# Where the convolution's matmul groups stand: gate chains, filter block 3 and block 2's inverse, and the order of the opening

## The chip, the cores and the metric

The kernel runs on one core of one Trainium2 chip. The metric is the device time of one execution in microseconds (us). Of the kernel before, three executions were timed, and one further execution was recorded by the hardware profiler. The engines are TensorE (PE in the profile, its weight loads PEld), VectorE (DVE), ScalarE (ACT), GpSimd (POOL) and SyncE (SP). Each runs its own instructions in program order and waits on semaphores for the others. POOL and SP also issue the DMAs.

## The reference

Two layers alternate, each a long convolution with a gate (A) and a GeGLU feed-forward (B), for 2048 tokens of width 576, hidden width 4608. Both layers use the same A_k, A_v and filters, so the convolution `y` is the same in both, and only its gate `q` differs. Abridged:

```python
def _A_ref(q, k, v, shift_k, ssm_k, ssm_D):
    k_shift = sum of k_pad[:, t:t+S, :] * shift_k[:, ks-1-t]        # ks = 4
    kv = k_shift * v
    y = irfft(rfft(pad(kv)) * rfft(pad(ssm_k)))[:S]                 # causal, length 2S
    return q * (y + kv * ssm_D)

def _B_ref(x, w_gate, w_up, w_down):
    return (gelu(x @ w_gate) * (x @ w_up)) @ w_down

x = A_q
for layer in range(2):
    x = x + _A_ref(layernorm(x), A_k, A_v, A_shift_k, A_ssm_k, A_ssm_D)
    x = x + _B_ref(layernorm(x), B_w_gate, B_w_up, B_w_down)
```

## The kernel before

**Units and visits.** Tokens are cut into four chunks c = 0 to 3 of 512. A unit is (layer, chunk), u0 = (0,0), u1 = (0,1), u2 = (1,0), u3 = (1,1), u4 = (0,2), u5 = (0,3), u6 = (1,2), u7 = (1,3). The feed-forward runs in five passes, [u0], [u1, u2], [u3, u4], [u5, u6], [u7], and each pass goes three times through a third of the hidden width. One third of one unit is called a visit here, numbered 0 to 23 in the order in which they run: u0 has visits 0 to 2; u1 and u2 alternate in 3 to 8, u3 and u4 in 9 to 14, u5 and u6 in 15 to 20; u7 has 21 to 23. A visit is first 216 matmuls for gate and up (`gu`, L1376, 12 tiles of 18), each tile followed by the gelu on ACT (L1380) and the product on DVE (L1381); then 96 matmuls down (`dn`, L1393), for each of the four token tiles j 24 of them, whose sum DVE adds to `x_c` (L1429, in a unit's last visit L1424 with a row sum, or L1415 into the output tile). PSUM has three buffers in pool `psp`, for `gu` and `dn`, and one in `cpsp`, for the convolution.

**The convolution** is a block transform of four blocks of 512 tokens, written as matmuls with twiddle tables `W` and `Wx`. Class `Conv` holds deques of its steps: `Pq` (matmul groups), `V` and `U` (DVE steps), `L` (loads and transposes). `filt(b)` transforms block b of the filter in eight small groups (`quarter`, L254: two matmuls into `cps`, then an ACT copy to an `eo` buffer, of which there are N_EO = 4); the DVE closures `both`, `even` and `odd` combine four `eo` buffers. `step(m)` does block m: the shift and product (`kv_ops`), its transform (again `quarter` for m > 1), the products with the filter blocks (`prod`, `add`), `cross` and `shift`, which writes `z` (L306), and the inverse, four groups of eight matmuls (`inverse`, L325) whose result ACT copies to `y` (L331). `self.neo` counts the `eo` buffers in use. In the program the order is filter 2, block 2, filter 3, block 3.

**The order around the feed-forward** is fixed when the program is built, by a planner with a clock for each engine (`Pace`: `t.pe`, `t.dve`, `t.act`, with costs such as `C_R4`). After each `gu` tile and each pair of `dn` matmuls it calls `fill(limit, tensor, conv_first)`, which issues loads, DVE steps, ACT steps (`aq`) and, where `tensor` is true, groups from `Pq` by `run_p`. `tensor` is true in the `dn` part, and in the `gu` part when `now()` says so.

**Gate chains.** When chunk c's `y` and `x` are there, the tasks of `prep` (deque `vq`) make the gate of the convolution layer and the next layer norm, for each of four tiles: `x_c` times gate (L1040, L1047 on DVE), mean (`nm`, L1004 on POOL), squares (`junk`, L1012 on ACT), `ve` and `rstd` (L1019, L1020 on POOL), the normed tile `xn` (L1073 on DVE), and two DMA transposes by SP into `xnT` (L1103), from which the unit's `gu` matmuls read. For a layer-1 unit the chain starts in the `dn` part of the layer-0 unit's last visit; for u4 and u5 it starts when block 2's or block 3's inverse is there.

**The opening** (`begin`, L674 to L884) is written out by hand: block 0 of filter and input, products `kacc(kt)` into `A[(part, kt)]`, sums and differences `pair0(kt, sg)` into `yb` (L799), four inverses `inv0(mt)` into PSUM tiles `Y[mt]`, then the gates of the first four tiles (`gate0`, L1236 and L1239), norms (L1189), PE transposes (`turn0`, L1205) and copies (`copy0`, L1212), up to the first `gu` matmul (L1308). `stats(j)` (L970 to L978) makes mean and variance of tiles 0 and 1 of `x_b`. SP issues the loads of the opening one after the other.

Of the kernel before, what the change touches and what calls it, by code (L numbers as in the profile page):

```python
# [17 lines left out]
F32 = mybir.dt.float32  # L18
# [4 lines left out]
P = 128  # L23
# [3 lines left out]
RT = BS // P  # L27
# [14 lines left out]
AHEAD = 3.0  # L42
# [41 lines left out]
class Conv:  # L84
# [9 lines left out]
    def __init__(self, tc, ctx, pace, A_k, A_v, A_shift_k, A_ssm_k, A_ssm_D, ident, psp, cpsp, ypool):  # L94
# [30 lines left out]
        self.h1_at = {2: 0.0}  # L125
        self.load_at, self.tight = -9.0, lambda: False
# [77 lines left out]
    def fwd_full(self, src, kt, s, dst, copy=None, ps=None):  # L204
# [6 lines left out]
        (copy or nc.scalar.copy)(out=self.halves(dst[:, s, :]), in_=ps[:, :, 0:HW])  # L211
# [13 lines left out]
    def quarter(self, src, out, h, ready, seen, done):  # L225
# [90 lines left out]
    def inverse(self, m, mt, terms, ps=None):  # L316
# [6 lines left out]
        for n, (lhs, z) in enumerate(terms):  # L323
            for h in range(2):
                nc.tensor.matmul(ps[:, h, 0:HW], lhsT=lhs, rhs=z[:, h * HW:(h + 1) * HW],  # L325
                                 start=(n == 0), stop=(n == len(terms) - 1))
# [41 lines left out]
    def filt(self, b):  # L368
# [23 lines left out]
        for h in range(2):  # L392
            self.Pq.extend(self.quarter(lambda: own["t"], out, h, lambda: own.get("at", NEVER), seen, done))

    def step(self, m, kv=None, loaded=False):
# [186 lines left out]
        for mt in range(RT):  # L582
            self.Pq.append((lambda: max(zs(), self.y_used.get(m - 2, NEVER) if m > 1 else 0.0), 0.98, inv(mt)))
# [34 lines left out]
    def run_p(self, other=False):  # L618
# [4 lines left out]
        ready, cost, run = self.Pq[0]  # L623
# [50 lines left out]
    def begin(self, head, tables):  # L674
# [4 lines left out]
        with ExitStack() as es:  # L679
# [88 lines left out]
            def h_part(b, kt, s, copy=None, ps=None):  # L768
# [7 lines left out]
                self.fwd_full(src, kt, s, t, copy, ps)  # L776
                if s == 1 and b == 0:
                    self.flush(0.0)
                    self.spill(self.Hd[b][kt], t)

# [26 lines left out]
            taps(DBS[0])  # L807
            turn_h(0, hT0, 0)
# [33 lines left out]
            head.stats(0)  # L842
# [3 lines left out]
            head.stats(1)  # L846
# [6 lines left out]
            h_part(1, 2, 0)  # L853
            self.flush(0.0)
# [629 lines left out]
```

## Time and profile before

| what | us |
|---|---|
| timed executions | 936.36, 938.77, 939.27 |
| median | 938.77 |
| profiled execution, its own time | 936.63 |
| its span | 934.9 |
| PE busy in it | 917.5 |
| DVE busy | 589.0 |
| ACT busy | 291.9 |
| POOL busy | 143.5 |

The span runs from the first to the last instruction; 1.7 us lie around it. In the profile's lines a matmul's duration is longer than the distance to the next one, since matmuls overlap; an idle time in square brackets is that of the engine just before the line's first instruction, with what ended it. Windows give the busy time of each engine in a stretch, and the clock that TensorE was granted as a share of full speed.

### The profile page before, as it was taken

Reading aid. Unit: us, or ns where it says so; the run is one execution under the profiler, and the core shown is the slowest. Engines: PE = TensorE matmul, PEld = TensorE weight load, DVE = VectorE, ACT = ScalarE, POOL = GpSimd, SP = SyncE. Lnnn points to the kernel's source line nnn. Section 1 sums busy time; section 2 is a strip of 40 time slices with the busy share of each in tenths; the row PEclk is TensorE's granted clock in tenths of the full one; section 3 lists DMA queues with packets and bytes.
Section 4 is the critical chain, followed back from the end, with each engine's and each line's share of the span. In section 5 each row is a group of like instructions: output and inputs, shape, how many; then the busy total and the mean of one; then the engine's idle time right before and its main releaser. Section 6 shows DMA issues by size and latency. Waiting matters only on the chain.

```text
span 934.9 us, 19345 instructions
## 1 busy us (share of the span) xinstructions
PE 917.5 (98%) x8248; PEld 536.7 (57%) x8249; DVE 589.0 (63%) x1051; ACT 291.9 (31%) x538; POOL 143.5 (15%) x305
## 2 busy tenths in 40 slices
PE   9899998999999999999999999899999999999998
PEld 6786555465565565664654655646556556556555
DVE  6888977677569888677698896653333335433332
ACT  6663224423224233332324122431221223311211
POOL 2433003201013131121014110320000002100000
PEclk9999999999999999999999999989999999999999
DMA  9978978909329717647725913650720730787720
GB/s 257 344 191 251 178 181 165 249 31 261 103 76 188 223 42 139 154 115 185 183 65 131 238 59 90 120 122 19 147 84 1 143 87 13 137 206 159 146 65 26
DMA packets 128490, 130.25 MB, mean 139 GB/s; under 512 B 43538, under 2 KB 120339, under 8 KB 128404
## 3 DMA queue, kind: packets, MB, share of 16 engines
q1 hardware_dynamic: 119232, 93.47, 46.6%
q0 software_dynamic: 9168, 35.54, 11.3%
q8 instruction: 64, 1.05, 0.5%
q14 instruction: 22, 0.18, 0.1%
q10 hardware_dynamic: 4, 0.01, 0.0%
HBM read 107.76 MB, written 11.80 MB: 128 GB/s over the span
## 4 chain that ended last, share of the span: by engine, by line
PE 93%; DVE 3%; POOL 2%; issue 1%; ACT 1%; DMA 0%; SPq 0%; DVEq 0%
PE gu L1376 58%; PE dn L1393 28%; PE gu L1308 3%; PE cps L325 1%; PE cps L254 1%; POOL rstd L1020 1%; PE cps L219 1%; DVE x_c L1424 0%; POOL ve L1019 0%; DVE yb L287 0%; ACT junk L1012 0%; POOL nm L1004 0%; DVE prod L286 0%; PE ps L209 0%; DVE yb L799 0%
## 5 line engine op out<-in xcount | busy, mean ns | idle before, releaser
L1376 PE MATMUL gu<-xnT,wgu 64*128 64x512 bf16 x4968 | 544.0, 377 | 5.9 <-DMA xnT<-xn 5.4
L1376 PEld LDWEIGHTS <-wgu 64*128 64x128 bf16 x4968 | 242.8, 94 | 300.3 <-issue 15.9
L1380 ACT ACTIVATE ga<-gu 128x512 f32<-128x512 f32 x276 | 164.8, 597 | 522.5 <-PE gu L1376 504.2
L1381 DVE TENSOR_TENSOR hT<-ga,gu 128x512 bf16<-128x512 f32 x276 | 189.2, 686 | 210.6 <-ACT ga L1380 209.4
L1393 PE MATMUL dn<-wd,hT 128*128 128x288 bf16 x2304 | 294.3, 286 | 0.5 <-DVE ob L1402 0.5
L1393 PEld LDWEIGHTS <-hT 128*128 128x128 bf16 x2304 | 223.5, 98 | 66.1 <-issue 10.5
L1429 DVE TENSOR_TENSOR x_c<-x_c,dn 128x576 f32<-128x576 f32 x64 | 48.1, 752 | 59.9 <-PE dn L1393 59.8
L1004 POOL TENSOR_SCALAR nm<-s 128x1 f32<-128x1 f32 x62 | 24.6, 397 | 299.3 <-DVE x_c L1424 170.2
L1012 ACT ACTIVATE junk<-x_c,nm 128x576 bf16<-128x576 f32 x48 | 37.0, 770 | 34.1 <-POOL nm L1004 34.0
L451 POOL DMA_DIRECT2D hr<-Hd x32 | 17.3, 542 | 149.9 <-DVE prod L286 149.9
L1020 POOL TENSOR_TENSOR rstd<-ve,neghalf_t 128x1 f32<-128x1 f32 x62 | 38.2, 617 | 5.2
L256 ACT COPY eo<-cps 128x576 f32<-128x576 f32 x32 | 20.4, 637 | 31.6 <-PE cps L254 31.6
L1415 DVE TENSOR_TENSOR ob<-x_c,dn 128x576 bf16<-128x576 f32 x15 | 11.3, 754 | 23.9 <-PE dn L1393 18.2
L1308 PE MATMUL gu<-xnT,wgu 64*128 64x256 bf16 x432 | 24.8, 269 | 0.5 <-DVE xnT L1212 0.5
L1308 PEld LDWEIGHTS <-wgu 64*128 64x128 bf16 x432 | 21.2, 94 | 3.5 <-issue 1.5
L287 DVE TENSOR_TENSOR prod<-prod 128x576 bf16<-128x576 bf16 x48 | 22.0, 458 | 1.7
L1019 POOL TENSOR_SCALAR ve<-ss 128x1 f32<-128x1 f32 x62 | 17.9, 289 | 30.8 <-ACT junk L1012 30.6
L1073 DVE TENSOR_SCALAR xn<-x_c,nm,rstd 128x576 bf16<-128x576 f32 x28 | 16.1, 576 | 4.5 <-POOL rstd L1020 4.4
L529 DVE TENSOR_TENSOR zs<-zs,prod 128x576 f32<-128x576 f32 x24 | 18.1, 754 | 0.3
L526 DVE TENSOR_TENSOR zs<-sum,prod 128x576 f32<-128x576 bf16 x24 | 18.1, 753 | 0.3
L184 DVE TENSOR_TENSOR kvt<-k,skc 128x1152 bf16<-128x1152 bf16 x24 | 17.7, 753 | 0.2
L340 POOL DMA_DIRECT2D out_dram<-ob x12 | 6.7, 556 | 72.8 <-DVE ob L1415 70.1
(138 smaller groups left out, 538.1 us busy)
## 6 DMA issues: line engine op xcount, KB each, us to landing
wgu<-in_B_w_gate_dram SPq DMA_DIRECT2D x45, 576.0 KB, 5.6
wd<-in_B_w_down_dram SPq DMA_DIRECT2D x30, 864.0 KB, 7.0
wgu<-in_B_w_up_dram SPq DMA_DIRECT2D x45, 512.0 KB, 7.9
hr<-Hd POOLq DMA_DIRECT2D x32, 288.0 KB, 5.5
kr<-Kd POOLq DMA_DIRECT2D x24, 288.0 KB, 6.0
Kd<-kc POOLq DMA_DIRECT2D x12, 288.0 KB, 4.5
k<-in_A_k_dram POOLq DMA_DIRECT2D x3, 1008.0 KB, 7.0
wgu<-in_B_w_up_dram SPq DMA_DIRECT2D x45, 64.0 KB, 7.3
```

The source lines that it names most:

```text
L256: nc.scalar.copy(out=A[i][:], in_=ps[:, :, 0:HW])
L287: nc.vector.tensor_tensor(out=dst, in0=pr[:, 0, :], in1=pr[:, 1, :], op=ALU.subtract if part == 0 else ALU.add)
L526: nc.vector.tensor_tensor(out=f[:], in0=self.halves(pr0[:]), in1=self.halves(pr[:]), op=ALU.add)
L1004: nc.gpsimd.tensor_scalar(out=v["nm"][:], in0=v["s"][:], scalar1=-1.0 / D, scalar2=None, op0=ALU.mult)
L1012: nc.scalar.activation(out=junk[:], in_=get_x(), func=ACT.Square, bias=v["nm"][:, 0:1], accum_out=v["ss"][:])
L1020: nc.gpsimd.tensor_tensor(out=v["rstd"][:], in0=ve[:], in1=neghalf_t[:, 0:1], op=ALU.pow)
L1308: nc.tensor.matmul(pair[:, s, e * 256:(e + 1) * 256], lhsT=w[r0:r0 + HK, k, gi * P:(gi + 1) * P], rhs=xnT[r0:r0 + HK, blk_of[k], tok], sta ...
L1376: nc.tensor.matmul(pair[:, s, :], lhsT=w[r0:r0 + HK, k, gi * P:(gi + 1) * P], rhs=xnT[r0:r0 + HK, b, :], start=(k == 0), stop=(k == NKC - 1))
L1380: nc.scalar.activation(out=ga[:], in_=pair[:, 0, :], func=ACT.Gelu_apprx_tanh)
L1381: nc.vector.tensor_tensor(out=hT[:, fi, :], in0=ga[:], in1=pair[:, 1, :], op=ALU.mult)
L1393: nc.tensor.matmul(acc[:, h, 0:HW], lhsT=hT[:, fi, at * P:(at + 1) * P], rhs=wd[2 * wb + fi // WT][:, fi % WT, h * HW:(h + 1) * HW], start ...
L1429: nc.vector.tensor_tensor(out=xh, in0=xh, in1=acc[:, :, 0:HW], op=ALU.add)
```

## The change

It has three parts.

1. **Groups and gate chains.** `fill` lets a group out of `Pq` only when the planner's clock is past `conv.ps_free`, and 2.5 us (`CHAINED`) past it while `chained()` holds, that is while ACT steps are queued or the head of `vq` is anything but a gate whose `y` is not there yet. The wait does not hold as long as block 1's inverse is not done. `conv.tight`, which spaces the loads, is the same test.
2. **Filter 3 ahead of block 2's inverse.** The four inverse groups of block 2 are kept in `self.then` and put into `Pq` behind filter 3's groups, which in turn wait until `z` of the block before is there (`z_at`). In `quarter` the groups come in the order 0, 1, 2, 3; the next four may start when two `eo` buffers are free again (`odd` and `even` give back two each, `odd` first), where before the first of them waited for all four. `wanted()` lets block 2's inverse out in the `gu` part too when the head of `vq` waits for it.
3. **Opening.** `x_b` is loaded ahead of `W` and `Wx` on SP's queue, and `stats(0)` and `stats(1)` come before the second shift product. `straight(mt)` forms inverses 0 and 2 from the products `A` themselves, six terms in place of four (12 matmuls in place of 8), and the first eight matmuls of inverse 0 come ahead of the filter's part `h_part(1, 2, 0)`. `pair0(1, 0)` is moved to the end of the opening. `Y[3]` goes to `psp` in place of `cpsp`, `h_part(1, 2, 0)` to `cpsp`, the DVE copy of `h_part(1, 2, 1)` is issued separately (`rest`), and the second transpose tile of `turn0` goes to `cpsp`.

```diff
-AHEAD = 3.0
+AHEAD, CHAINED = 3.0, 2.5
...
         def even():
...
+            self.neo -= 2
             done(0, h, t.on_dve(2 * C_R4) + LAG)
         def odd():
...
-            self.neo -= RT
+            self.neo -= 2
...
+                    self.U.append((when + LAG, 4 * C_BF, odd))
                     self.U.append((when + LAG, 2 * C_R4, even))
-                    self.U.append((when + LAG, 4 * C_BF, odd))
...
-        return [(lambda i=i: max(ready(), NEVER if self.neo >= (N_EO if i else 1) else 0.0), 0.25, one(i)) for i in (0, 2, 1, 3)]
+        return [(lambda: max(ready(), NEVER if self.neo >= N_EO else 0.0), 0.25, one(i)) for i in range(RT)]
...
-            self.Pq.extend(self.quarter(lambda: own["t"], out, h, lambda: own.get("at", NEVER), seen, done))
+            self.Pq.extend(self.quarter(lambda: own["t"], out, h, lambda: max(own.get("at", NEVER), self.z_at[b - 1]()), seen, done))
+        self.Pq.extend(self.then)
+        self.then = []
...
-        for mt in range(RT):
-            self.Pq.append((lambda: max(zs(), self.y_used.get(m - 2, NEVER) if m > 1 else 0.0), 0.98, inv(mt)))
+        self.z_at[m] = zs
+        out = [(lambda: max(zs(), self.y_used.get(m - 2, NEVER) if m > 1 else 0.0), 0.98, inv(mt), m) for mt in range(RT)]
+        if m == 2:
+            self.then = out
+        else:
+            self.Pq.extend(out)
...
             self.load_v(0, nc.sync)
+            head.more(0)
             nc.sync.dma_start(out=self.W[:, 0:12, :], in_=tables[:, 0:12, :])
             nc.sync.dma_start(out=self.Wx[:], in_=tables[:, 24:26, :])
-            head.more(0)
...
+            def straight(mt):
+                w, odd = self.inv_w, [(s, kt) for kt in (1, 3) for s in range(2)]
+                return [(w(mt, s), self.yb[(s, 0, 0)]) for s in range(2)] + [(w(mt, s, mt == 2), A[(s, kt)]) for s, kt in odd]
...
             taps(DBS[0])
+            head.stats(0)
+            head.stats(1)
             turn_h(0, hT0, 0)
...
             pair0(0, 0)
-            head.stats(0)
             tile(1)
             kacc(1)
             pair0(0, 1)
-            head.stats(1)
             tile(3)
...
             kacc(3)
-            h_part(1, 2, 0)
-            self.flush(0.0)
-            pair0(1, 0)
             Y = {mt: self.psp.tile([P, 2, 512], F32, tag="pr", name="ps") for mt in (2, 1, 0)}
             small = lambda: self.cpsp.tile([P, 2, 512], F32, tag="cps", name="cps")
-            inv0(0, Y[0])
-            inv0(2, Y[2])
+            near = {mt: straight(mt) for mt in (0, 2)}
+            self.inverse(0, 0, near[0][:4], Y[0], True, False)
+            h_part(1, 2, 0, None, small())
+            self.flush(0.0)
             pair0(1, 1)
+            self.inverse(0, 0, near[0][4:], Y[0], False, True)
+            self.inverse(0, 2, near[2], Y[2])
+            rest = h_part(1, 2, 1, nc.vector.tensor_copy, small(), True)
             inv0(1, Y[1])
             head.gate(0, Y[0])
             head.mean(0)
             self.keep_y(0, 2, Y[2])
-            self.keep_y(0, 1, Y[1])
+            Y[3] = inv0(3, self.psp.tile([P, 2, 512], F32, tag="pr", name="ps"))
...
             self.keep_y(0, 3, Y[3])
+            pair0(1, 0)
             self.startup = False
...
+    def chained():
+        need = vq[0][0] if vq else None
+        return bool(aq) or need is not None and not (need[0] == "y2" and need[1:3] not in conv.y_at)
...
-        if tensor:
+        if tensor and (hurry() or t.pe > conv.ps_free + (CHAINED if chained() else 0.0)):
             for _ in range(3):
                 if not conv.run_p():
                     break
...
-            pt.append(new() if two else pt[0])
+            pt.append(cpsp.tile([P, 2, 1024], BF16, tag="cps", name="xps") if two else pt[0])
...
-        now = lambda: hurry() and (t.pe > 60.0 or conv.fresh > 0)
-        conv.tight = lambda: bool(vq or aq)
+        def wanted():
+            need = vq[0][0] if vq else (None,)
+            return conv.Pq and len(conv.Pq[0]) > 3 and need[0] == "y2" and need[1:3] not in conv.y_at
+        now = lambda: wanted() or hurry() and (t.pe > 60.0 or conv.fresh > 0)
+        conv.tight = chained
```

In the built program the change moves matmuls as follows, against the order before. In visit 2's `dn` part one of three filter groups (L254) is left, after 74 of the 96 `dn` matmuls; the two others come in visit 3. Block 2's transform ends in visit 4 (before: visit 5). Filter 3's groups come in visits 7 and 8 (before: 8 and 9), block 2's inverse stays in visit 8, behind them. Block 3's transform comes in visits 8 and 9 (before: 10), and block 3's inverse in visit 13 (before: visit 14). On DVE block 3's last `z` stands ahead of nine of the twelve L1381 of visit 13. On SP's queue u5's eight transposes now come in visit 14, ahead of two sets of gate and up weights (L944 to L946) that stood before them. On POOL's queue the first six loads of block 3's products (`kr`, `hr`) stand ahead of and between the first steps (`nm`, `ve`, `rstd`) of u4's chain.

More of the change, by code (lines that the diff above doesn't have):

```diff
@@ L125, in __init__ @@
         self.h1_at = {2: 0.0}
+        self.z_at, self.then = {}, []
         self.load_at, self.tight = -9.0, lambda: False
@@ L202, in kv_ops, with fwd_full @@
         return ops
-    def fwd_full(self, src, kt, s, dst, copy=None, ps=None):
+    def fwd_full(self, src, kt, s, dst, copy=None, ps=None, later=False):
         nc = self.nc
@@ L210, in fwd_full @@
                                  start=(n == 0), stop=(n == RT - 1))
-        (copy or nc.scalar.copy)(out=self.halves(dst[:, s, :]), in_=ps[:, :, 0:HW])
+        run = lambda: (copy or nc.scalar.copy)(out=self.halves(dst[:, s, :]), in_=ps[:, :, 0:HW])
+        return run if later else run()
     def fwd_eo(self, src, kt, s, h, scale=1.0):
@@ L314, in terms, with inverse @@
         return out + [(w(mt, 0, mt == 1), z[(1, 1, sg)]), (w(mt, 1, mt == 3), z[(0, 1, sg)])]
-    def inverse(self, m, mt, terms, ps=None):
+    def inverse(self, m, mt, terms, ps=None, first=True, last=True):
         nc = self.nc
@@ L325, in inverse @@
                 nc.tensor.matmul(ps[:, h, 0:HW], lhsT=lhs, rhs=z[:, h * HW:(h + 1) * HW],
-                                 start=(n == 0), stop=(n == len(terms) - 1))
+                                 start=(first and n == 0), stop=(last and n == len(terms) - 1))
         if own:
@@ L622, in run_p @@
             return False
-        ready, cost, run = self.Pq[0]
+        ready, cost, run = self.Pq[0][:3]
         if max(ready(), 0.0 if other else self.ps_free) > t.pe:
@@ L766, in begin, with h_part @@
             h0, kc, A = {}, {}, {}
-            def h_part(b, kt, s, copy=None, ps=None):
+            def h_part(b, kt, s, copy=None, ps=None, later=False):
                 if b == 1:
@@ L775, in h_part @@
                     t, src = h0[kt], hT0
-                self.fwd_full(src, kt, s, t, copy, ps)
+                run = self.fwd_full(src, kt, s, t, copy, ps, later)
                 if s == 1 and b == 0:
```

7 lines of the change are left out of this document (4 added, 3 removed).

## The prediction, made before the changed kernel had run

> **What bounds the kernel now.** The page comes first: span, engines, clock.
>
> ```profile
> span 934.9 us, 19345 instructions
> PE 917.5 (98%) x8248; PEld 536.7 (57%) x8249; DVE 589.0 (63%) x1051; ACT 291.9 (31%) x538; POOL 143.5 (15%) x305
> ...
> PEclk9999999999999999999999999989999999999999
> ```
>
> TensorE is the bound almost everywhere; DVE has over a third of its time free. So the change can win only where PE stands idle or runs slowly, and it wins nothing by moving matmuls about. There are 17.4 us of idle PE in the span, and one slice whose clock is below 9. I then read PE's timeline around each idle time, and the chain of waits for the length of an undisturbed visit. The largest is at the start of visit 15, u5's first:
>
> ```profile
> 596.31 8.00 PE L1393 MATMUL dn<-wd,hT 128*128 128x288 bf16 x64
> 609.27 0.61 PE L1376 MATMUL gu<-xnT,wgu 64*128 64x512 bf16 x2 [4.95 <-DMA xnT<-xn]
> 610.34 4.02 PE L1376 MATMUL gu<-xnT,wgu 64*128 64x512 bf16 x18 [0.46 <-DMA xnT<-xn]
> ```
>
> ```profile
> 565.11 23.42 PE gu L1376 x216
> ...
> 636.25 11.87 PE dn L1393 x96
> ```
>
> The `dn` matmuls end at 596.31 + 8.00 = 604.31, and the next `dn` part begins at 636.25, so visit 15's 216 `gu` matmuls took 31.94 where 23.42 is usual: **8.52 us lost**. Only 5.41 of it is idle time. The rest is the clock:
>
> ```profile
> core 0: us, PE busy (x) PEld busy (x) DVE busy (x) ACT busy (x) POOL busy (x), PEclk, DMA share, GB/s
> 604.30:609.30 5.00, 0.05 (x3) 0.06 (x2) 2.90 (x7) 1.15 (x4) 2.85 (x7) 0.96 0.54 106
> 609.30:614.00 4.70, 4.24 (x20) 1.65 (x22) 0.00 (x0) 0.00 (x0) 0.00 (x0) 0.50 0.86 249
> 614.00:618.00 4.00, 4.00 (x32) 1.79 (x30) 2.75 (x5) 2.49 (x5) 0.89 (x3) 0.78 0.53 177
> 160.00:166.00 6.00, 3.07 (x26) 2.14 (x26) 4.07 (x9) 3.16 (x7) 3.85 (x9) 1.00 0.92 179
> ```
>
> After the idle time TensorE is granted half speed (0.50, then 0.78). Its cause is that block 3's inverse runs only in visit 14, the last before u5 starts, so u5's whole gate chain and eight transposes are squeezed into one `dn` part, beside u6's.
>
> The second idle time stands in visit 2:
>
> ```profile
> 159.53 1.14 PE L1393 MATMUL dn<-wd,hT 128*128 128x288 bf16 x8
> 163.61 0.40 PE L254 MATMUL cps<-hT,W 128*128 128x288 bf16 x2 [2.93 <-ACT eo L256]
> ```
>
> ```profile
> 162.17 0.78 ACT L1012 ACTIVATE junk<-x_c,nm 128x576 bf16<-128x576 f32 x1 [2.81 <-POOL nm L1004]
> ...
> 162.94 0.62 ACT L256 COPY eo<-cps 128x576 f32<-128x576 f32 x1
> ```
>
> A filter group waits for the one `cps` buffer. Its copy stands on ACT behind a `junk` that waits 2.81 us for u2's gate chain. The clock stayed at 1.00 (last row of the windows), so this one costs its 2.93 and no more.
>
> [...]
>
> **Term 1: block 3's inverse a visit earlier.** In the built order it stands in visit 13, 35.3 us (23.42 + 11.87) earlier, and DVE's last `z` nine tiles of visit 13, some 17 us, ahead of it. u5's gates then stand in the `gu` part of visit 14, as u4's do in visit 9 (386 to 422) now, where PE is busy throughout:
>
> ```profile
> 386.00:422.00 36.00, 36.00 (x322) 20.38 (x320) 27.07 (x51) 12.73 (x24) 9.82 (x22) 1.00 0.52 136
> ```
>
> The eight transposes end over 10 us before visit 15. So the 8.52 go. What is late next is u6's chain, alone now, in visit 14's `dn` part. Its DVE order is the one that u7's chain has now in visit 19, so I take that row's price, **+0.49**:
>
> ```profile
> 793.73 6.63 PE L1376 MATMUL gu<-xnT,wgu 64*128 64x512 bf16 x59 [0.49 <-DVE x_c L1424]
> ```
>
> Bounds: 0 and 2.93, the other chain's wait. No matmul is added in the visits. By counting each visit's DVE instructions at their durations, the fullest visit has about 30 us of DVE work after the change and 29 before, of 35.3. That cover holds both the earlier products and the hT products on which PE waits.
>
> **Term 2: fewer groups in visit 2's `dn` part.** One of three is left, and its buffer was freed long before. PE then reaches visit 3 2.93 earlier, near 163.0. What could be late there is u1's `xnT`, or the tile buffer that the last L1424 frees:
>
> ```profile
> 155.50 3.89 SPq L1103 DMA_TRANSPOSE xnT<-xn  x3
> ...
> DMA to landing us min/median/max: 2.5/3.5/6.0
> ```
>
> ```profile
> 162.18 0.75 DVE L1424 SCALAR_TENSOR_TENSOR x_c<-dn,x_c 128x576 f32<-128x576 f32 x1
> ...
> 163.27 0.82 DVE L1040 SCALAR_TENSOR_TENSOR g_t<-x_c,nm,y 128x576 f32<-128x576 f32 x1 [0.33 <-POOL nm L1004]
> ```
>
> The third transpose is issued near 158.1 and lands at 161.6 by the median, 164.1 by the worst. The fourth tile's L1424 follows the L1040 at 163.27 and ends near 164.8; the third `gu` tile needs that buffer at 163.0 + 2 × 1.95 = 166.9. So **-2.93**, at worst -1.8. The two groups moved to visit 3 cost PE the same there as here.
>
> **Term 3: the opening.** DVE sets the pace from 18 us to the first gates.
>
> ```profile
> 28.41 0.81 DVE L970 BATCH_NORM_STATS2 stats<-x_b 128x6 f32<-128x288 bf16 x2
> ...
> 29.62 0.75 DVE L283 TENSOR_TENSOR prod<-kc,h 128x1152 bf16<-128x1152 bf16 x1
> ...
> 32.01 1.56 DVE L799 TENSOR_TENSOR yb<-yb 128x576 bf16<-128x576 bf16 x4
> 33.49 0.81 DVE L1236 SCALAR_TENSOR_TENSOR x_c<-x_b,mv,ps 128x576 f32<-128x576 bf16 x1
> ...
> 39.39 0.57 DVE L1189 TENSOR_SCALAR xn<-x_c,nm,rstd 128x576 bf16<-128x576 f32 x1
> ```
>
> ```profile
> 27.65 0.64 ACT L211 CAST kc<-ps 128x576 bf16<-128x576 f32 x1 [0.34 <-PE ps L209]
> 28.52 2.14 ACT L764 COPY hT<-hps 128x1152 bf16<-128x1152 bf16 x2 [0.24 <-PE hps L763]
> 34.31 0.65 ACT L331 ACTIVATE y<-ps 128x576 bf16<-128x576 f32 x1 [2.03 <-PE ps L325]
> ```
>
> ```profile
> 27.45 2.03 PE L763 MATMUL hps<-ident,hn 128*128 128x128 bf16 x20
> ...
> 41.14 1.08 PE L1308 MATMUL gu<-xnT,wgu 64*128 64x256 bf16 x14 [0.45 <-DVE xnT L1212]
> ```
>
> Two statistics of 1.21 us each (28.41 to 29.62) leave this stretch. The last products (29.62) cannot follow by 2.42, since their input is copied at 27.65 + 0.64 = 28.29; they start at 28.33 and end at 30.80 (2.47 later, as 29.62 to 32.09 now). PE: transposes end at 29.48; eight matmuls of inverse 0 at 0.122 each (from the 64 of the same shape in 8.00, whose last ends 0.29 after its start) end at 30.46; the filter part's eight wait for the second `hT` copy (30.66) and end at 31.45; the four last of inverse 0 end near 32.1. So the first L1236 starts at 32.15 in place of 33.49. Inverse 2's twelve end near 33.6, its `y` copy at 34.3 in place of 34.96, and the second gate starts 0.8 earlier. From there nm, squares and `rstd` follow as now; the second L1189 waits for its `rstd` near 38.45 in place of 39.39, and transposes, copies and the first L1308 follow 0.94 earlier: **-0.94**. The eight matmuls added lie in idle PE time ahead of that gate. Without that cover they cost 0.98. `Y[3]` in `psp` holds the third `gu` tile alone, whose buffer is copied out by then. Bounds: +0.5 (the copies in the new ACT order late) and -1.34 (what the first gate gains).
>
> The moved loads and statistics lie before:
>
> ```profile
> 9.55 1.22 DVE L755 TENSOR_TENSOR v<-ps,v 128x1024 bf16<-128x1024 f32 x1 [2.00 <-PE ps L639]
> 13.27 1.22 DVE L755 TENSOR_TENSOR v<-cps,v 128x1024 bf16<-128x1024 f32 x1 [2.49 <-PE cps L639]
> ```
>
> ```profile
> 0.00:10.00 10.00, 8.26 (x56) 5.30 (x57) 4.94 (x14) 4.46 (x8) 1.26 (x8) 1.00 0.80 277
> 13.71 1.15 PE L219 MATMUL ps<-hT,W 128*128 128x288 bf16 x8
> ```
>
> DVE idles 2.49 there, and both statistics take 2.42. `x_b` (576 KB) at 277 GB/s takes 2.1 us, by which `W` lands later; it is first used at 13.71, and `kc`'s matmuls use the second product only after L219. I take 0 for both.
>
> **Sum.** 936.63 - 8.52 + 0.49 - 2.93 - 0.94 = 924.7, against the profiled execution. That one lies 2.1 under the median of the runs shown (938.77), of which one is as fast. The half-speed stretch, which need not be equally long in each run, goes away, so I add only 0.5: **925.2**. By the bounds its own range is 923.5 to 928.5.
>
> **Rivals.**
>
> *The filter groups find a new wait* (0.13). Groups of four now overlap: the next four write `eo` buffers that `odd` and `even` must free, and an ACT copy that waits holds gelus and the `cps` buffer. Against it: the waits list has PE waiting for L256 once in all.
>
> ```profile
> POOL hr L451 <- DVE prod L286: 149.9, 19, 31.8
> ...
> PE cps L254 <- ACT eo L256: 2.9, 1, 2.9
> ```
>
> Two such waits give 924.7 + 5.9 = 930.6; four, 936, no change.
>
> *Term 2 does not come* (0.09): PE reaches visit 3 earlier and stands there for u2's chain instead. 925.2 + 2.9 = 928.1. For it, the row at 793.73, where the same L1424 did hold PE. Against it, 2.1 us of margin.
>
> *Slower* (0.08). On POOL's queue three pairs of `kr` and `hr` loads now stand ahead of u4's `nm`. Such a load holds POOL until a product on DVE has freed a buffer, up to 31.8 us at once (first row above). ACT's `junk` then waits with gelus behind it, and PE has three tiles, 5.9 us, in hand. At 31.8 PE loses 26, and 925.2 + 26 = 951. It decides from a wait of 5.9 + 11.9 = 18 us. Against it: three buffers of each kind were freed by block 2's last products, a visit before.
>
> **How the numbers follow.** Forecast 0.70, rivals 0.13, 0.09 and 0.08. 0.3%, 2.8 us, is about what a measurement can tell. Faster: 0.70 + 0.09 + 0.10 of the first rival = 0.89; the same 0.03; slower 0.08. The range 923 to 931 holds the forecast, the second rival and the smaller half of the first.
>
> **What would show it.** PE without the idle 2.93 near 160 and the 4.95 near 600, and PEclk 9 in every slice; L325's third set in visit 13; the first L1308 near 40.2; at visit 15's start at most half a microsecond's wait. Wrong: a PE wait for L256 or for hT in visits 3 to 9, `nm` late in visit 9, or L219 waiting for `W`.

## The result and the profile after

| | before | after |
|---|---|---|
| median of the runs timed together, us | 937.75 (936.36 to 939.27, 4 runs) | 929.41 (928.35 to 930.52, 4 runs) |
| profiled execution: time, span, us | 936.63, 934.9 | 928.90, 927.1 |

The ratio is 0.9911, with a 95% interval of 0.9888 to 0.9934: 8.3 us, 0.9%, faster, where 925.2 (12.6 under the 937.75) had been forecast. The direction was right; a third of the gain is missing. The page of the changed kernel begins so:

```profile
span 927.1 us, 19363 instructions
...
PE 915.8 (99%) x8257; PEld 538.3 (58%) x8257; DVE 589.8 (64%) x1051; ACT 292.0 (31%) x538; POOL 142.0 (15%) x305
...
PEclk9999999999999999999999999999999999999999
```

The slice with 8 in PEclk is gone, and PE's idle time falls from 17.4 us to 11.3. The two large waits are no longer there. First PE's timeline at the end of visit 2 (start, length, instructions, and in brackets the idle time before them), then at the start of visit 15 with the windows over it:

```profile
158.47 0.41 PE L257 MATMUL cps<-hT,W 128*128 128x288 bf16 x2
158.71 2.86 PE L1420 MATMUL dn<-wd,hT 128*128 128x288 bf16 x22
161.50 1.69 PE L1403 MATMUL gu<-xnT,wgu 64*128 64x512 bf16 x14
```

```profile
604.30 4.06 PE L1403 MATMUL gu<-xnT,wgu 64*128 64x512 bf16 x36
608.87 19.60 PE L1403 MATMUL gu<-xnT,wgu 64*128 64x512 bf16 x180 [0.51 <-DVE x_c L1451]
```

```profile
604.30:609.30 5.00, 4.49 (x41) 1.99 (x42) 3.41 (x8) 2.98 (x7) 2.55 (x7) 1.00 1.16 123
```

One filter group and no wait in visit 2; at visit 15 no wait for `xnT`, a clock of 1.00, and 0.51 for u6's chain. The new losses are seen by comparing parts. PE is busy almost without a break, so a part's length, from its first matmul to the next part's first, shows every delay. Undisturbed it is 23.42 for `gu` and 11.87 for `dn`, plus 0.245 for each filter or transform group and 0.98 for each inverse group that stands in a `dn` part. (In a `gu` part an inverse group takes 1.19: visit 2's four make it 28.18 long in both kernels.) What is beyond that is called the excess here. All parts whose excess the change altered, and the opening (visit 20's `gu` part keeps the excess of 0.67 that it had):

| part | before: length, excess | after: length, excess | change, us |
|---|---|---|---|
| first `gu` matmul of the kernel | 41.14 | 40.35 | -0.79 |
| visit 2 `dn` | 15.69, 3.09 | 12.11, 0 | -3.09 |
| visit 14 `dn` + visit 15 `gu` | 47.72, 8.51 | 35.97, 0.68 | -7.83 |
| visit 3 `dn` | 13.09, 0 | 14.00, 0.42 | +0.42 |
| visit 4 `dn` | 13.34, 0 | 15.34, 1.51 | +1.51 |
| visit 8 `gu` | 23.42, 0 | 23.83, 0.41 | +0.41 |
| visit 8 `dn` | 16.77, 0 | 18.12, 0.86 | +0.86 |
| visit 9 `dn` | 12.85, 0 | 14.09, 0.75 | +0.75 |
| sum | | | -7.76 |

The spans differ by 7.74. So the three steps of the change brought 11.71, and five new delays in visits 3 to 9 took back **3.95**. PE's part of the list of waits names them (total, times, longest). The three waits of the first row stand in visits 3, 4 and 9 (0.26, 1.35 and 0.59); of the second row only 0.24, in visit 8, belongs to the new delays, and the others are those of visits 15 and 20; the third row is visit 8's:

```profile
PE cps L257 <- ACT eo L259: 2.2, 3, 1.3
...
PE gu L1403 <- DVE x_c L1451: 1.3, 3, 0.5
...
PE cps L257 <- DVE v L195: 0.7, 1, 0.7
```

The dearest is in visit 4. DVE's, ACT's and PE's timelines of the changed kernel there:

```profile
225.16 0.76 DVE L286 TENSOR_TENSOR prod<-kr,hr 128x1152 bf16<-128x1152 bf16 x1 [1.40 <-DMA hr<-Hd]
...
228.22 0.75 DVE L236 TENSOR_TENSOR eo<-eo 128x576 f32<-128x576 f32 x1
...
231.81 1.56 DVE L249 TENSOR_TENSOR kc<-eo 128x288 bf16<-128x288 f32 x4
```

```profile
226.71 0.64 ACT L259 COPY eo<-cps 128x576 f32<-128x576 f32 x1 [0.59 <-PE cps L257]
233.46 0.64 ACT L259 COPY eo<-cps 128x576 f32<-128x576 f32 x1 [6.11 <-DVE kc L249]
```

```profile
231.17 0.41 PE L257 MATMUL cps<-v,W 128*128 128x288 bf16 x2
231.41 1.39 PE L1420 MATMUL dn<-wd,hT 128*128 128x288 bf16 x10
234.15 0.41 PE L257 MATMUL cps<-v,W 128*128 128x288 bf16 x2 [1.35 <-ACT eo L259]
```

The first four groups have filled the four `eo` buffers by 227.35. DVE has stood 1.40 us for an `hr` load, until 225.16. It then does the products and `x_c`, starts on the sums of the four buffers (L236) only at 228.22, and ends `odd` (L249) at 233.37. Only then can ACT copy the fifth group, and the sixth stands on PE behind that copy, because there is one `cps` buffer.

The kernel before has eight groups at the same distances in visit 10, and there nobody waits for a buffer. PE's, DVE's and ACT's timelines of the kernel before:

```profile
449.30 0.41 PE L254 MATMUL cps<-v,W 128*128 128x288 bf16 x2
...
454.20 0.41 PE L254 MATMUL cps<-v,W 128*128 128x288 bf16 x2
```

```profile
447.97 0.76 DVE L234 TENSOR_TENSOR eo<-eo 128x576 f32<-128x576 f32 x1 [1.17 <-ACT eo L256]
```

```profile
454.65 0.64 ACT L256 COPY eo<-cps 128x576 f32<-128x576 f32 x1 [4.26 <-PE cps L254]
```

The fifth group follows the fourth by 4.90 us there (449.30 to 454.20), as it does in the changed kernel's visit 4 (226.27 to 231.17). But DVE starts on the sums 2.60 us after the start of the `dn` part (445.37), in the changed kernel 5.88 us after it (222.34). So it is not the distance of the groups that makes the wait of visit 4, but how late DVE is with the buffers.

In visit 8 another thing is late: DVE waits 3.59 us for the load of `v`, which takes 10.0 us from issue to landing, and two transform groups wait for DVE's last product with it.

```profile
383.08 0.76 DVE L195 TENSOR_TENSOR v<-kvt,v 128x1152 bf16<-128x1152 bf16 x1 [3.59 <-DMA v<-in_A_v_dram]
```

### The profile page after: what moved, and what is told of

Read it like the earlier page. It is cut to its first block, busy times and chain, and to the rows that moved or that the text cites. A ratio compares the mean times of both kernels' runs of the same rounds, so it can differ in the third digit from the quotient of the medians.

```text
span 927.1 us, 19363 instructions
## 1 busy us (share of the span) xinstructions
PE 915.8 (99%) x8257; PEld 538.3 (58%) x8257; DVE 589.8 (64%) x1051; ACT 292.0 (31%) x538; POOL 142.0 (15%) x305
## 4 chain that ended last, share of the span: by engine, by line
PE 87%; DVE 4%; issue 3%; DMA 3%; POOL 2%; ACT 1%; DVEq 0%; ACTq 0%; POOLq 0%
PE gu L1403 53%; PE dn L1420 25%; PE gu L1331 3%; POOL rstd L1038 1%; DMA v<-in_A_v_dram 1%; PE ps L210 1%; PE cps L328 1%; DMA hr<-Hd 1%; DMA Hd<-hc 1%; PE cps L221 1%; PE cps L257 1%; DVE x_c L1451 1%; ACT junk L1030 1%; PE cps L210 1%; POOL ve L1037 0%
## 5 line engine op out<-in xcount | busy, mean ns | idle before, releaser
L1022 POOL TENSOR_SCALAR nm<-s 128x1 f32<-128x1 f32 x62 | 22.7, 367 | 313.8 <-DVE x_c L1451 207.6
L1442 DVE TENSOR_TENSOR ob<-x_c,dn 128x576 bf16<-128x576 f32 x15 | 11.3, 753 | 30.9 <-PE dn L1420 24.7
L1065 DVE SCALAR_TENSOR_TENSOR x_c<-g_t,rstd,x_c 128x576 f32<-128x576 f32 x16 | 13.1, 817 | 12.8 <-POOL rstd L1038 12.7
```

Source lines behind the costliest of these rows:

```text
L1022: nc.gpsimd.tensor_scalar(out=v["nm"][:], in0=v["s"][:], scalar1=-1.0 / D, scalar2=None, op0=ALU.mult)
```

## The experiments

The question had three parts: whether the three gains come from the three steps; what makes the five new delays; and why runs of one kernel differ by up to 4 us. All lengths below are of parts, as in the table. Experiments 1 to 8 and 11 are one profiled execution each, so they are read by their parts and not by their times.

**1. The opening alone** (the rules for groups, the priority of the inverse and the filter order as before; beside the lines shown, the order of the groups in `quarter` and what `even` and `odd` give back are also as before).

```diff
...
-        if m == 2:
-            self.then = out
-        else:
-            self.Pq.extend(out)
+        self.Pq.extend(out)
...
-        if tensor and (hurry() or t.pe > conv.ps_free + (CHAINED if chained() else 0.0)):
+        if tensor:
...
-        now = lambda: wanted() or hurry() and (t.pe > 60.0 or conv.fresh > 0)
-        conv.tight = chained
+        now = lambda: hurry() and (t.pe > 60.0 or conv.fresh > 0)
+        conv.tight = lambda: bool(vq or aq)
```

> The opening alone: the groups, the gates' priority and the filter order are those of the kernel before. Theory (the opening's 0.8 us are a gain of its own, and what follows moves with it): first gu matmul at 40.3 us as in the changed kernel, visit 2's dn part 15.7 us and visit 15's stall as in the kernel before, span 934.9 - 0.8 = 934.1 us. Rival (the gain is swallowed by the wait in visit 2, whose end is set by the gate chain and not by PE): visit 2's dn part 16.5 us, span 934.9 us.

Neither came. The first `gu` matmul is at 41.29, 0.15 later than before, and the span is 936.5. Visit 2's `dn` part is 17.16 us, with the same idle time as before (2.94). What is new stands in the windows of this run behind that idle time (length, busy times of PE, PEld, DVE, ACT and POOL, granted clock, DMA share, GB/s):

```profile
160.80:163.70 2.90, 0.00 (x0) 0.00 (x0) 2.48 (x7) 1.41 (x4) 0.98 (x5) 0.94 1.05 230
163.70:167.10 3.40, 3.37 (x16) 2.14 (x16) 2.02 (x3) 1.35 (x3) 3.04 (x5) 0.55 1.19 184
```

The same wait that left the clock at 1.00 in the profile of before here cost a half clock, 17.16 - 15.69 = 1.47 us more. Visit 15's stall is as before (`gu` part 26.92), as expected. None of the five new delays is there: they come with the rules for the groups and not with the opening. And the opening begins differently in each profile: from the first matmul of L221 (before: L219) to the first `gu` matmul it takes 26.70 to 26.72 us in the eleven profiles of the new opening, and 27.43 in both of the old (the second is experiment 11). So the rewritten stretch gains **0.72**; what stands ahead of it varies by more.

**2. Without the condition that keeps groups clear of gate chains.**

```diff
-        if tensor and (hurry() or t.pe > conv.ps_free + (CHAINED if chained() else 0.0)):
+        if tensor:
...
-        conv.tight = chained
+        conv.tight = lambda: bool(vq or aq)
```

> The changed kernel without its condition that keeps groups clear of gate chains (and with the old rule for the spacing of POOL's loads); three filter groups stand in visit 2's dn part again. Theory (the number of groups beside the chain makes the wait): PE waits near 160 us for the eo copy for 2.5 to 3 us, span 927.1 + 2.9 = 930.0 us. Rival (the new order of the groups and their buffers removed the wait): no wait there, span 927 us. On the new waits of visits 3, 4, 8 and 9 (0.4 + 1.5 + 1.3 + 0.8 us): if the spacing of POOL's loads makes them they go, if the groups' own order does they stay.

The theory holds for visit 2's wait, not for the span, which is 932.9: the first `gu` matmul is 1.64 us later than in the changed kernel, and the clock cost more in visit 2. PE's timeline of this run:

```profile
160.36 1.14 PE L1420 MATMUL dn<-wd,hT 128*128 128x288 bf16 x8
164.45 0.40 PE L257 MATMUL cps<-hT,W 128*128 128x288 bf16 x2 [2.95 <-ACT eo L259]
```

With three groups the wait is back at 2.95, though the rest of the change is there. The part is 17.38 us long, since the clock falls here too (0.50 from 166 to 168 us). Of the new delays visits 8 and 9 keep theirs (18.10 and 14.09 in the `dn` parts), visit 4 has an excess of 0.37 in place of 1.51 and visit 3 one of 0.87 in place of 0.42. So the new spacing of POOL's loads does not make the delays of visits 8 and 9. For visits 3 and 4 the run cannot say, since it takes back two rules at once.

**3. Block 3's inverse held back to visit 14.**

```diff
-        out = [(lambda: max(zs(), self.y_used.get(m - 2, NEVER) if m > 1 else 0.0), 0.98, inv(mt), m) for mt in range(RT)]
+        out = [(lambda: max(zs(), NEVER if m == 3 and self.visit < 14.5 else 0.0, self.y_used.get(m - 2, NEVER) if m > 1 else 0.0), 0.98, inv(mt), m) for mt in range(RT)]
...
+            conv.visit = n_visit
...
+            conv.visit += 0.5
             for j in range(RT):
                 acc = psp.tile([P, 2, 512], F32, tag="pr", name="dn")
```

> The changed kernel with block 3's inverse held back until visit 14's dn part; everything else in its order stays. Theory (the place of the inverse alone makes the stall before visit 15): idle of 4.5 to 5.5 us before visit 15's first gu matmul, a granted clock near 0.5 behind it, span 927.1 + 7.8 = 935 us. Rival (the stall came from the crowd on DVE in visits 9 to 14, which the new filter order has thinned): idle of 1 to 3 us, clock 1.00, span 929 to 931 us.

The place alone brings the stall back, larger than before. PE's timeline of this run:

```profile
589.49 1.14 PE L328 MATMUL cps<-yb,W 128*128 128x288 bf16 x8
...
600.27 1.14 PE L328 MATMUL cps<-yb,W 128*128 128x288 bf16 x8
601.25 3.84 PE L1422 MATMUL dn<-wd,hT 128*128 128x288 bf16 x30
614.50 0.61 PE L1404 MATMUL gu<-xnT,wgu 64*128 64x512 bf16 x2 [9.41 <-DMA xnT<-xn]
```

The kernel before has the four inverse groups 6.6 us from first to last (588.72 to 595.33, the same view of it); here it is 10.8. What is new about them is the rule that keeps groups clear of gate chains; by the code it holds the inverse groups apart as well, though no run of its own shows that this alone does it. The last group comes 4.2 us later and the idle time grows by 4.5. The clock is 0.50 behind the idle time (614.5 to 618), and visit 15's `gu` part is 26.57 long, span 939.8.

**4 and 5. Matmuls in the idle time.** In two versions of experiment 3, 64 and 150 transposes fill part of the stall (here 150; the edit of experiment 3 stands beside it).

```diff
+            if n_visit == 15:
+                still = cpsp.tile([P, 2, 1024], BF16, tag="cps", name="still")
+                for _ in range(150):
+                    nc.tensor.transpose(still[:, 0, 0:P], ident[:], ident[:])
```

> As the kernel with the inverse held back until visit 14's dn part, plus 64 transposes of the identity into a PSUM tile that nobody reads, ahead of visit 15's first gu matmul (some 4 us of PE work in the idle time). Theory (the idle time makes the half clock): granted clock 1.00 around it, the wait for xnT as long as without them, span 3.1 us less than that kernel's, 932 us. Rival (the clock falls there for another reason, or those transposes end too late): clock 0.5 again or gu delayed, span 935 us or more.

> As the kernel with the inverse held back and 64 transposes, but with 150 of them, 8.8 us of PE work in an idle time of 9.4. Theory (the idle time makes the half clock): granted clock 1.00 there, visit 15's gu part 23.9 us in place of 26.6, its start not later than 614.5 less the difference of the openings. Rival (the clock falls for another reason): gu part near 26.5 us.

With 64 it says nothing on the question: 5.84 us stayed idle behind them, the clock fell (0.50 from 613.6 to 618), the `gu` part was 26.36 and the span 938.7. With 150, by timeline and windows:

```profile
604.35 8.54 PE L1366 MATMUL still<-ident 128*128 128x128 bf16 x150
615.08 5.21 PE L1408 MATMUL gu<-xnT,wgu 64*128 64x512 bf16 x44 [2.19 <-DMA xnT<-xn]
```

```profile
615.10:618.00 2.90, 2.79 (x26) 1.44 (x28) 0.00 (x0) 0.41 (x1) 0.00 (x0) 1.00 0.71 189
```

The clock stays at 1.00 and the `gu` part takes 23.71, 2.86 less than in experiment 3, of which 0.47 is a second wait for `xnT` that no longer stands by itself. Its first matmul came 1.2 us later after the start of the `dn` part than there, which was not expected and stays unexplained. That leaves 1.7 of the 2.86; the span is 2.3 shorter (937.5), the rest by smaller delays in visits 4 and 8. So the clock stayed at 1.00 in the one profile whose stall was filled but for 2.19 us. In five 5.4 us or more stayed idle at this place: in both of before and in experiments 3 and 4 the window behind it shows 0.50 to 0.58, and experiment 1, which has no window there, has a part as long as the first profile's (26.92, 26.91). Here the idle time makes the half clock.

**6. Loads told to the planner as later.**

```diff
-                at["v"] = t.pe + 9.0
+                at["v"] = t.pe + 11
...
-                    at[("ld", kt, a)] = t.pe + 8.0
+                    at[("ld", kt, a)] = t.pe + 10
...
-                at[("ld", kt, a)] = t.pe + 8.0
+                at[("ld", kt, a)] = t.pe + 10
```

> The changed kernel with the planner told that the loads land later: kr and hr 10 us after their issue (8 before), v 11 us (9 before). Theory (the new waits of visits 3, 4 and 8 come from loads that the planner takes for landed, so that a product stands on DVE ahead of odd, or a filter group ahead of v): PE's waits for the eo copy in visit 4 (1.35 us) and for v in visit 8 (0.69 us) go, span 927.1 - 2 = 925 us against the changed kernel's opening. Rival (the waits are those of groups that run faster than DVE can free their buffers, whenever the loads land): waits of the same sum at the same or other places, span 927 us.

The rival came. The wait in visit 4 shrinks to 0.71, the one for `v` goes, and others grow: the excess is 1.27 in visit 3, 0.87 in visit 4, 0.62 and 0.75 in visit 8 and 0.37 in visit 9, together 3.9 where the changed kernel has 3.95. The span is 928.1, with the first `gu` matmul 0.89 later than there. DVE still stands 0.99 us for `hr` in visit 4, so the load's lateness is made smaller and not taken away. In the list of waits of this run:

```profile
PE cps L257 <- ACT eo L259: 2.4, 3, 1.1
```

**7. `even` ahead of `odd`.**

```diff
-                    self.U.append((when + LAG, 4 * C_BF, odd))
                     self.U.append((when + LAG, 2 * C_R4, even))
+                    self.U.append((when + LAG, 4 * C_BF, odd))
```

> The changed kernel with even ahead of odd on DVE, as the kernel before has it. Theory (the fifth group's copy waits for the buffers that odd frees, so what stands ahead of odd adds to the wait): PE's wait for the eo copy in visit 4 grows from 1.35 by the 1.54 us of even to about 2.9 us. Rival (the copy waits for something else on ACT or for the load alone): 1.35 us as before. Visits 7 to 9 have another order of groups here and are not compared.

Neither came: the wait in visit 4 is split, and the excess there is 1.29 in place of 1.51. ACT's timeline of this run:

```profile
233.29 0.64 ACT L259 COPY eo<-cps 128x576 f32<-128x576 f32 x1 [4.64 <-DVE kc L242]
...
236.98 0.64 ACT L259 COPY eo<-cps 128x576 f32<-128x576 f32 x1 [1.92 <-DVE kc L249]
```

The fifth copy waits for `even` (L242) and the seventh for `odd`; PE loses 0.37 and 0.59. So the fifth copy isn't tied to `odd`: in both runs it takes the pair of buffers that comes free first, and here the pair that is served last holds up a later copy. The planner also placed the products after the sums here, so that no `hr` wait stands ahead of them, and order and load weren't told apart. The span is 928.1, with the first `gu` matmul 1.21 later than in the changed kernel.

**8. Buffers counted as free only when DVE is nearly through with them.**

```diff
-AHEAD, CHAINED = 3.0, 2.5
+AHEAD, CHAINED, EO_LAG = 3.0, 2.5, -1.0
...
-            self.neo -= 2
-            done(1, h, t.on_dve(4 * C_BF) + LAG)
+            when = t.on_dve(4 * C_BF) + LAG
+            self.eo_late.append((when + EO_LAG, 2))
+            done(1, h, when)
...
-        return [(lambda: max(ready(), NEVER if self.neo >= N_EO else 0.0), 0.25, one(i)) for i in range(RT)]
+        return [(lambda: max(ready(), NEVER if self.eo_used() >= N_EO else 0.0), 0.25, one(i)) for i in range(RT)]
+
+    def eo_used(self):
+        while self.eo_late and self.eo_late[0][0] <= self.t.pe:
+            self.neo -= self.eo_late.popleft()[1]
+        return self.neo
```

(`even` likewise)

> The changed kernel with a group's buffers counted as free 1 us before DVE is through with them, by the planner's clock, in place of at the issue of odd and even; the transform of block 2 moves mostly to visit 5, and block 3's inverse to visit 14's gu part. Theory (the new waits are those for eo buffers, and visit 14's gu part is early enough for u5's chain): the waits of visits 3, 4 and 9 go (2.2 us), visit 15's first gu part stays near 24.1 us, span 925 us. Rival (an inverse in visit 14 is too late): a wait of 1 us or more at visit 15's start, span 928 us or more.

Neither came as described; the span is 946.4. Visit 4, with two groups in place of eight, has no excess, visit 3's grows from 0.42 to 1.57, and block 2's inverse slips to visit 9, where PE's timeline has:

```profile
427.66 0.64 PE L259 MATMUL cps<-v,W 128*128 128x288 bf16 x2 [1.65 <-ACT eo L261]
439.88 2.73 PE L1410 MATMUL gu<-xnT,wgu 64*128 64x512 bf16 x11 [11.59 <-DMA xnT<-xn]
```

The gates for the next pass then end too late, and PE stands 11.59 us. Holding groups back costs some 19 us where 2.2 were to be won. One part of the theory came: block 3's inverse stands in visit 14's `gu` part here, and visit 15's `gu` part is 24.12, as in the changed kernel. The delays must be removed without moving block 2's inverse.

**9. Five `eo` buffers.** Every engine runs its instructions in the same order as in the changed kernel.

```diff
-        self.prp = pool("c_pr", 3)
+        self.prp = pool("c_pr", 2)
...
-        self.eop = pool("c_eo", N_EO)
+        self.eop = pool("c_eo", 5)
```

> The changed kernel with five eo buffers in place of four, paid for with one of the three product buffers that DVE alone writes and reads; the order of instructions is the same on every engine. Theory (the new waits of visits 3, 4 and 9 are those of a group's copy for a buffer that odd must free): PE's waits for the eo copy there, 0.26 + 1.35 + 0.59 us, fall to at most 0.2 in all, visit 4's dn part from 15.3 to 14.0 us; visit 8's waits (for v, for u3's chain) stay; span 927.1 - 2.2 = 924.9 us for an opening like the changed kernel's. Rival (the copy waits for DVE or ACT in some other way, or the next group waits in its turn): the dn parts of visits 3, 4 and 9 as long as in the changed kernel.

The theory holds. Visits 3, 4 and 9 have `dn` parts of 13.58, 14.22 and 13.34, an excess of 0, 0.39 and 0. Visit 8 keeps its two. The span is 924.9 with the first `gu` matmul at 40.41. Waits of PE in this run, and ACT's timeline in visit 4:

```profile
PE cps L257 <- DVE v L195: 0.6, 1, 0.6
...
PE cps L257 <- ACT eo L259: 0.2, 1, 0.2
```

```profile
231.26 0.64 ACT L259 COPY eo<-cps 128x576 f32<-128x576 f32 x1 [4.26 <-PE cps L257]
233.21 0.64 ACT L259 COPY eo<-cps 128x576 f32<-128x576 f32 x1 [1.32 <-DVE kc L249]
```

The fifth copy now waits for PE's matmuls alone; the sixth is the one that waits for L249, and it costs 0.23.

**10. Five buffers, and `v` told to the planner as later.**

```diff
-                at["v"] = t.pe + 9.0
+                at["v"] = t.pe + 13.0
```

(beside the edit of experiment 9)

> The same with five eo buffers, and with the planner told that v lands 13 us after its issue (9 before), so that the two transform groups of visit 8 move to visit 9. Theory: besides the eo waits visit 8's wait for v, 0.69 us, goes, and visit 9 takes eight groups without a wait; span 924.2 us for an opening like the changed kernel's, the fastest of all. Rival (visit 9 has no room for eight groups, or block 3's products come later for it): a wait for eo or kc of 0.6 us or more in visit 9, span 924.9 us or more.

The theory holds: the list of waits has no row of PE for `eo` or `v` any more, visit 8's `dn` part is 16.77 and visit 9's, with eight groups, 13.83, both without excess. The span is 923.8 with the first `gu` matmul at 40.56. Over five runs it takes 927.02 us (925.63 to 927.25), ratio to the kernel before 0.9886 (0.9867 to 0.9906); experiment 9 has 927.16 (926.66 to 927.59, 4 runs), 0.989 (0.9871 to 0.9909). Both medians lie 2.2 us or more under the changed kernel's 929.41 of another batch, and every run of theirs lies under its lowest. But the kernel before was 0.8 us faster too in the later batch (936.91 over 9 runs, in place of 937.75), and the intervals of the ratios overlap with the changed kernel's 0.9888 to 0.9934. That the delays are gone is read from the parts; the gain in time is likely and not settled. Which of the two is better, the times don't tell either.

**11. The kernel before once more.**

> The kernel before once more, unchanged, for its clock. [...]

Both waits, visit 2's and visit 15's, are there with nearly the same idle time, and at visit 15 the clock differs. Visit 2's part is 15.70, as in the first profile; the first `gu` matmul is at 41.76, 0.62 later; and visit 15's `gu` part is 25.48 in place of 26.91. PE's timeline and the window of this run:

```profile
609.90 0.51 PE L1376 MATMUL gu<-xnT,wgu 64*128 64x512 bf16 x2 [4.96 <-DMA xnT<-xn]
610.97 5.27 PE L1376 MATMUL gu<-xnT,wgu 64*128 64x512 bf16 x36 [0.56 <-DMA xnT<-xn]
```

```profile
609.90:614.00 4.10, 3.54 (x20) 1.52 (x22) 0.00 (x0) 0.00 (x0) 0.00 (x0) 0.58 0.82 218
614.00:618.00 4.00, 4.00 (x40) 1.99 (x37) 2.84 (x5) 2.70 (x6) 0.75 (x3) 1.00 0.72 247
```

Nearly the same idle time (5.52 here, 5.41 in the first profile) cost 25.48 - 23.42 - 0.56 = 1.50 us of clock here and 3.03 there, and the program is the same. For visit 2 the run says nothing new: its clock stayed at 1.00 in both.

## Why the prediction was right or wrong

- **Term 1 (-8.52, +0.49): right.** It measured -8.51 and +0.68; the wait for u6's chain is the 0.51 at 608.87. The 0.49 was an idle time, and the row that it was taken from costs 0.67 as the excess of its part (visit 20), so the wait came as foreseen and its price was read 0.2 too low. Experiment 3 shows that the inverse's place decides it, experiment 5 that the part beyond the idle time is the clock. That part is between 1.5 and 3.0 us by the run, and the sum took the upper end, the profile's; that the profile of before happened to have it is luck, and experiment 11 shows the other end.
- **Term 2 (-2.93): right.** It measured -3.09, and the rival that PE would stand in visit 3 instead did not come: visit 3's `gu` part is 23.42. In experiment 2, with the two rules taken back and three groups beside the chain, the wait returns. "This one costs its 2.93 and no more" held for the two profiles of before that there are; in experiments 1 and 2 the same wait cost 1.5 to 1.7 more.
- **Term 3 (-0.94): right in kind, 0.2 too much.** The stretch that was rewritten gains 0.72; the difference of the two profiles, 0.79, has a little luck in it. The first and second gates came within 0.1 of what was worked out (32.06 and 34.28). The step that missed is the second L1189: its `rstd` was there at 38.41, as foreseen, but the third gate stood ahead of it on DVE until 38.59. The moved loads and statistics, taken as 0, show nothing that can be told from the variation ahead of L221.
- **What failed: the filter and transform groups at nothing.** The prediction let the groups cost PE "the same there as here" and gave the new wait, its first rival, a chance of 0.13, with the argument that PE waited for the copy once in all before. That list holds for places where DVE was early, and the runs showed DVE late at the new ones.

  In visit 10 of the kernel before, eight groups at the same distances had no wait: the first pair of buffers was free at 453.30, ahead of the fifth copy (454.65). The new rule lets the fifth group go as soon as one pair is planned to be free, not when it is. In visit 4 `odd` ended 6.0 us after the fourth copy, because DVE came late to the sums, behind products and the 1.40 for `hr`. The new order of the groups may add to it: by the code the first sums need groups 0 and 2, which is the third copy now and was the second before, and in visit 3, where no load is late, DVE idles from 187.9 to 188.8 while the third copy ends at 188.71. How much each makes is open, since no run changes one of them alone. In experiment 7, without the products ahead, PE's wait at the sixth group is 0.37 in place of 1.35. What is shown is that these are waits for a buffer: three of them made 2.7 (0.42 + 1.51 + 0.75), and experiment 9 took them away but for 0.39 by one buffer. The price of a single wait was taken as 2.93; the largest was 1.51.

  The remaining 1.3 is in visit 8: a load of 10.0 us that the planner puts at 9 (0.86), which experiment 10 removed by moving its two groups to visit 9, and 0.41 for u3's chain, which stayed. That one is an order on DVE. The last `x_c` of visit 7 (L1451), which frees the buffer for a `gu` tile, stands behind a gate step that waits for `rstd`; in the kernel before it stood ahead of that step (L1424 at 346.70, the gate step at 348.96). DVE's timeline of the changed kernel:

```profile
347.24 0.82 DVE L1065 SCALAR_TENSOR_TENSOR x_c<-g_t,rstd,x_c 128x576 f32<-128x576 f32 x1 [1.53 <-POOL rstd L1038]
...
347.99 0.75 DVE L1451 SCALAR_TENSOR_TENSOR x_c<-dn,x_c 128x576 f32<-128x576 f32 x1
```

  Experiment 8 has the same order and the same 0.42 without a filter group in visit 7, so the groups there don't make it. No run changes this order alone.
- **Against the sum:** forecast -11.9 to the profiled execution, measured -7.7; the terms were 0.2 too high and the waits 3.95 too low. Without the waits for buffers and `v` the sum nearly holds: experiment 10's profiled execution takes 925.6 us, against 924.7. It is the lowest of five, and their median, 927.0, is 1.8 over the 925.2. The 0.5 added for the half-speed stretch was the author's estimate, which no run shows; shown is that the stretch differs between executions, by 1.50 and 3.03 us of clock in the two profiles of before. The changed kernel's 929.41 lies outside the 923.5 to 928.5 that the bounds of the terms gave, and inside 923 to 931, which was made wide enough for half of the first rival. That rival's "two such waits" gave 930.6: near the time, and by its mechanism in 2.7 of the 3.95, three smaller waits in place of two. That their sum is near the price of two is luck. The sign of being wrong that the prediction named, a wait of PE for this copy in visits 3 to 9, was there.
- **The slower rival** (POOL's loads ahead of u4's `nm`): did not come. The loads take 0.5 to 0.6 us each on POOL in visit 9, and POOL waits for DVE and not for a load's buffer when the first `nm` starts, 5.2 us into the visit as before. POOL's timeline of the changed kernel:

```profile
391.68 0.22 POOL L1022 TENSOR_SCALAR nm<-s 128x1 f32<-128x1 f32 x1 [1.69 <-DVE x_c L1065]
```

## What to carry to other kernels

When a change moves work that goes through few buffers, count for each buffer who frees it, and place that engine's real lateness at the new place (its waits for loads too) against the time at which the buffer is wanted again: a list of waits of the old order can't show the wait that the new order makes. One more buffer, taken from a pool whose writer and reader are the same engine, removed a delay (2.7 us but for 0.39, experiment 9) that the three changes of order in experiments 6 to 8 did not. And a planner that counts a buffer as free when the freeing work is issued, not done, doesn't see such a wait.

## What the hardware showed that was not expected

In these profiles the length of the idle time alone does not settle whether the clock falls. An idle time of 2.93 to 2.95 us in visit 2 left the clock at 1.00 in two profiles and took it to 0.50 in two (experiments 1 and 2), for 1.5 to 1.7 us more. No one kernel showed both, so that the run and not the kernel decides is shown for visit 15, where one program lost 3.03 us and 1.50 (experiment 11), and only likely for visit 2. An idle time of 5.4 to 5.5 us stood at visit 15 in three profiles. Behind it the windows show 0.50 and 0.58 in the two of before, and experiment 1 is read by its part (26.92); the clock cost 1.5 to 3.0 us.

The opening differs from run to run as well. Two timelines of PE, of the changed kernel and of experiment 2, with the same instructions:

```profile
7.14 2.30 PE L648 MATMUL ps<-dg,kT 128*128 128x512 bf16 x14
9.27 2.04 PE L772 MATMUL hps<-ident,hn 128*128 128x128 bf16 x20
```

```profile
7.33 3.60 PE L648 MATMUL ps<-dg,kT 128*128 128x512 bf16 x14
10.72 2.23 PE L772 MATMUL hps<-ident,hn 128*128 128x128 bf16 x20
```

The fourteen matmuls take 2.30 us in one and 3.60 in the other. The granted clock stands at 1.00 in both, so the cause is not shown. What is seen is the pace: from 7.2 to 8 us PE has 4 matmuls in both, from 8 to 9 us 11 in the changed kernel and 6 in experiment 2. The first `gu` matmul falls between 40.35 and 41.99 in the eleven profiles of the new opening. Together, opening (1.6), visit 2 (1.7) and visit 15 (1.5) are large enough for the spread of the kernel before, 935.73 to 939.82 in the later runs; that they make it is not shown, since only two of its executions were profiled. The changed kernel has lost the two long waits, and its four runs lie within 2.2 us.
